# Cosine attention and an MLP mixer on one core: regrouped early slots, epsilon as a two-column sum, zero blocks on GpSimd, and channel weights in pieces of another shape

## The chip, the core and the metric

One core of one Trainium2 chip runs the kernel. The metric is the device time of one execution in microseconds (us). Six runs of the kernel before took 402.56 to 405.12 us, median 404.44 us. In the text TensorE is PE, VectorE is DVE, ScalarE is ACT, GpSimd is POOL and SyncE is SP, as the profile names them.

## The reference, cut to what matters

```
# q, k, v: (8, 12, 448, 64) float32;  tau = 0.1
q_n = q / (norm(q, axis=-1) + 1e-06)
k_n = k / (norm(k, axis=-1) + 1e-06)
attn = softmax(q_n @ k_n.T / tau)
x = (attn @ v) -> (8, 448, 768)              # the 12 heads side by side
h = relu(x.T @ w_tok1) @ w_tok2              # 448 -> 256 -> 448
u = x + h.T
out = u + relu(u @ w_ch1) @ w_ch2            # 768 -> 1536 -> 768
```

The change touches the norms, the epsilon that is added to them, the scaling of q and k, the load of `w_ch1`, and the order of work while the first batch is in flight.

## The kernel before, in words

The work is cut into 48 pairs of heads, six for each of the eight batches. Pair i is handled in slot i, and a slot works on several pairs at once: it scores pair i, multiplies the softmax of pair i-1 with v, runs the token mixer for older pairs, and prepares q and k of later ones. Slots 0 to 5 belong to batch 0, where the sequence is laid out as 112 partitions by 4 chunks. Slot 6 is written out by hand, and slots 7 to 47 run in a loop; from pair 6 on k and v are laid out as 128 rows by 3 chunks and a rest of 64 rows (`kr`, `vr`), which two heads share.

The order of work on every engine is the order in which the program is written: each engine runs its own instructions in that order, and waits at each for what it needs. What a pair goes through:

- `load_qk`, `load_v` (SP): loads in float32. SP is one queue too; it also issues the transposing DMA of `tok2` (line 399) that makes `ut` out of `u` for pairs 0, 1 and 2.
- `square` (POOL or ACT), `sums` (line 253, DVE): squares and their sum over the 64 elements of a row.
- `norms`: Ln and Exp on ACT give the square root; then either DVE adds epsilon (line 262) and takes the reciprocal (line 263), or, with `act=True`, ACT does both by two more activations (lines 268, 269). The early slots use DVE.
- `scale` (line 280): q and k times the reciprocal norm, into the float16 tile `kq`; on POOL except for the first pairs. From pair 6 on the rest of k takes two more multiplications of 64 partitions by 64 elements (line 288), into a block of zeros that DVE sets for pairs 6 to 9 (line 285).
- `tpose` (line 304, PE, and a copy to `qk` by DVE, line 306), or from pair 12 on a transposing DMA.
- `score` (line 327, PE; the exponential on ACT, line 328), `pv` (line 366; division on DVE, lines 369 and 370), `tok1`, `tok2` (PE; DVE lines 382 and 396), `upose` (line 405, PE, for pairs 3 to 5), and `warm`, which are matmuls without a use of their own.
- `m_ch1` (line 415), `m_ch2` (line 430): the channel mixer. From slot 7 on these units fill PE between the other steps, from a queue with a share for each slot. That share is worked out from column counts when the program is built. The first one needs `ut` of all six pairs of batch 0.

PSUM tiles come from two rings in the order in which they are asked for: tag "s" has three buffers (scores, and the token mixer where `wide`), tag "b" has two (transposes, `pv`, `warm`, `upose`). `kq` has four buffers. The weights `w_ch1` (768 by 1536 float32, stored as float16 in `wc1t`) come by four DMAs that POOL issues in slots 2 to 5, each of all six row tiles by 384 columns; the first unit of the channel mixer needs columns 0 to 127 of all row tiles. `w_ch2` comes by two DMAs of six row tiles by 768 columns each, issued in slot 8.

Of the kernel before, what the change touches and what calls it, by code (L numbers as in the profile page):

```python
# [22 lines left out]
def kernel(  # L23
# [169 lines left out]
                              in_=w2n[:].rearrange("p t (s c) -> p t c s", c=NCH))  # L193

    def weights_ch1(i):
        lo, hi = 384 * i, 384 * (i + 1)
        nc.gpsimd.dma_start(out=wc1t[:, :, lo:hi],
                            in_=moe_w_ch1[:, lo:hi].rearrange("(t p) c -> p t c", p=128))

    def weights_ch2():  # L200
        for i in range(2):
# [6 lines left out]
    sqs = [cst.tile([128, 2 * QS, E], FP32, name=f"sq{i}") for i in range(3)]  # L208
    for kq in kqs:
        nc.vector.memset(kq[96:128, 1].rearrange("p c g e -> p (c g e)"), 0.0)  # L210
    for sq in sqs:
        nc.vector.memset(sq[96:128, KS:KS + QS].rearrange("p c e -> p (c e)"), 0.0)

# [42 lines left out]
    def norms(i0, i1, a0=0, a1=2, dve=False, act=False):  # L256
        h = i0 // HP
        n, sl = some(i0, a0, a1)
        ssq = half[h]["ssq"][0:n, i0 - HP * h:i1 - HP * h, sl]
        rn = half[h]["rn"][0:n, i0 - HP * h:i1 - HP * h, sl]  # L260
        if dve:
            nc.vector.tensor_scalar_add(out=rn, in0=rn, scalar1=EPS_NORM)  # L262
            nc.vector.reciprocal(out=rn, in_=rn)
            return
        nc.scalar.activation(out=rn, in_=ssq, func=AF.Ln, bias=tiny[0:n])
        nc.scalar.activation(out=rn, in_=rn, func=AF.Exp, scale=0.5)
        if act:
            nc.scalar.activation(out=rn, in_=rn, func=AF.Ln, bias=eps[0:n])
            nc.scalar.activation(out=rn, in_=rn, func=AF.Exp, scale=-1.0)  # L269

    def scale(i, a, eng=None):
        st = pipe[i]
        eng = eng or nc.gpsimd
        sl, np_ = lay(i)
        if "kq16" not in st:
            st["kq16"] = kqs[i % 4]
        kq, p = st["kq16"], np_[a]
        rn = half[i // HP]["rn"][:, i % HP, sl[a]]
        n = KC if a == 0 and not old(i) else NCH
        eng.tensor_tensor(out=kq[0:p, a, 0:n].rearrange("p c g e -> p g c e"),  # L280
                          in0=st["kq"[a]][:].rearrange("p (g c) e -> p g c e", g=2),
                          in1=_bcast_free(rn[0:p, 0:2 * n].rearrange("p (g c) -> p g c", g=2), E), op=ALU.mult)
        if n == KC:
            if i < NPAIR + 4:
                nc.vector.memset(kq[:, 0, KC].rearrange("p g e -> p (g e)"), 0.0)
            for g in range(2):
                p = slice(64 * g, 64 * g + 64)
                eng.tensor_tensor(out=kq[p, 0, KC, g], in0=half[i // HP]["kr"][p, i % HP],
                                  in1=_bcast_free(rn[p, 2 * KC], E), op=ALU.mult)

    def scaled(i):
        scale(i, 0)
# [195 lines left out]
    with tc.manual_schedule():  # L488
        for i in range(3):
            load_qk(i)  # L490
        load_v(0)
        load_qk(3)
        load_v(1)
        load_qk(4)
        load_v(2)
        load_qk(5)
        load_v(3)
        weights_tok1()
        weights_tok2()

        square(0, 1, act=True)
        square(0, 0, act=True)
        sums(0, 1, 2)
        norms(0, 1, 1, 2)
        sums(0, 0, 1)
        norms(0, 1, 1, 2, dve=True)
        norms(0, 1, 0, 1)
        scale(0, 1, nc.vector)
        norms(0, 1, 0, 1, dve=True)
        scale(0, 0, nc.vector)  # L510
        square(1, 1, act=True)
        square(1, 0, act=True)
        square(2, 1, act=True)
        warm(40, True)
        tpose(0, 1, 2)
        warm(3, True)
        tpose(0, 0, 1)
        warm(5, True)
        square(2, 0)
        sums(1)  # L520
        score(0, 0)
        norms(1, 2)
        norms(1, 2, dve=True)
        score(0, 1)
        scale(1, 0)
        scale(1, 1, nc.vector)
        sums(2)
        cast_v(0)
        score(0, 2)
        warm(14)  # L530
        score(0, 3)
        warm(6)
        tpose(1)
        warm(6)
        norms(2, 3)
        norms(2, 3, dve=True)
        square(3, 1, act=True)
        square(3, 0)
        load_v(4)
        load_qk(6)  # L540

        for i in range(1, NPAIR + 1):
            b, pj = i // NPAIR, i % NPAIR
            if i < NPAIR:
                if i == 1:
                    scale(2, 0)
                    scale(2, 1, nc.vector)
                else:
                    scaled(i + 1)
                    weights_ch1(i - 2)  # L550
                score(i, 0)
                score(i, 1)
                sums(i + 2)
                norms(i + 2, i + 3)
                if i >= 2:
                    tok1(i - 2, wide=True)
                pv(i - 1, 0)
                norms(i + 2, i + 3, dve=True)
                cast_v(i)
                square(i + 3, 0)  # L560
                if i == 1:
                    warm(10)
                tpose(i + 1)
                score(i, 2)
                if i >= 2:
                    tok2(i - 2, pe=(i == NPAIR - 1), wide=True)
                pv(i - 1, 1)
                score(i, 3)
                warm(8)
                square(i + 3, 1, act=True)  # L570
                if i == 1:
                    place_w2()
                load_v(i + 4)
                load_qk(i + 6)
                continue
            load_qk(12)
            load_qk(13)
            scaled(7)
            score(i, 0)
            score(i, 1)  # L580
            sums(8)
            norms(8, 9)
            score(i, 2)
            upose(i - 3)
            tok1(i - 2, wide=True)
            pv(i - 1, 0)
            norms(8, 9, dve=True)
            cast_v(i)
            load_v(i + 4)
            squares(9)  # L590
            score_rest(i)
            tpose(i + 1)
            pv(i - 1, 1)
            tok2(i - 2, pe=True)
            tok1(i - 1, wide=True)
            tok2(i - 1, pe=True)

        def side(i):
            early = i < 12
            if i + 7 < NP_ALL:  # L600
                load_qk(i + 7)
            if i == 8:
                weights_ch2()
            cast_v(i)
            if i + 4 < NP_ALL:
                load_v(i + 4)
            if early:
                for t in SU_AT[i]:
                    sums(t)
                for n in sorted({t // HP for t in SU_AT[i]}):  # L610
                    ts = [t for t in SU_AT[i] if t // HP == n]
                    norms(ts[0], ts[-1] + 1, act=True)
                for t in SC_AT[i]:
                    scaled(t)
                    if t >= DMA_T0:
                        tpose_dma(t)
            for t in SQ_AT[i] if early else [i + 5]:
                if t < NP_ALL:
                    squares(t)
            if not early:  # L620
                if i + 4 < NP_ALL:
                    sums(i + 4)
                    if (i + 4) % HP == 2:
                        norms(i + 2, i + 5, act=True)
                if i + 2 < NP_ALL:
                    scaled(i + 2)
                    tpose_dma(i + 2)
        for i in range(NPAIR + 1, NP_ALL):
            b, pj = i // NPAIR, i % NPAIR
            for c in range(KC):  # L630
                score(i, c)
            pv_rest(i - 1)
            pv(i - 1, 0)
            pv(i - 1, 1)
            if i == NPAIR + 1:
                upose(NPAIR - 2)
                upose(NPAIR - 1)
                refill(0)
            elif pj == 2 and b > 1:
                refill(b - 1)  # L640
            side(i)
            fed[0] += fed[1]
            unit(True)
            score_rest(i)
            if i > NPAIR + 1:
                tok2(i - 2)
            if i + 1 < DMA_T0:
                tpose(i + 1)
            if due():
                unit(True)  # L650
            while due():
                unit()
            tok1(i - 1)
        last = NP_ALL - 1
        pv_rest(last)
        pv(last, 0)
        pv(last, 1)
        tok2(last - 1)
        unit()
        tok1(last)  # L660
        unit()
        tok2(last)
        refill(B - 1)
        while queue:
            unit()
# [35 lines left out]
```

## Time and profile before

| what | value |
|---|---|
| median of six runs | 404.44 us (402.56 to 405.12) |
| the profiled execution | 402.56 us, span 400.7 us |
| PE busy | 377.8 us, 94% of the span |
| DVE, ACT, POOL busy | 211.5, 227.2, 235.5 us (53%, 57%, 59%) |
| chain that ended last, by engine | PE 80%, DVE 8%, DMA 4%, ACT 4%, POOL 2% |
| time of the slots' first score | slot 1 14.5, slot 2 19.6, slot 3 25.0, slot 4 29.7, slot 5 34.5, slot 6 39.6, slot 7 46.5, slot 8 55.3, slot 9 65.7 us |
| data moved | 65.26 MB, HBM read 43.45 MB |

The profile's page gives the busy share of each engine over the span, then the same in 40 slices of 10 us, then DMA queues, then the chain of work that ended last. A line of the timeline has the start and the length in us, the engine, the line of the kernel, the operation with output and inputs, and in brackets the idle time of the engine before it with the operation that ended that idle time. Where several are merged, the length is that of all. Lengths of neighbours overlap a little, so the distance of two starts is what an instruction costs its engine.

### The profile page before, as it was taken

What the parts mean: (1) busy time and instruction counts of PE and PEld (TensorE: products, weight loads), DVE (VectorE), ACT (ScalarE), POOL (GpSimd) and SP (SyncE); (2) the same over time, 40 slices, a digit from 0 to 9 for tenths busy, and PEclk for the clock granted to TensorE, in tenths of its full rate; (3) what the DMA queues carried; (4) which work ended last, traced back from release to release, by engine and by line L of the source; (5) the groups of instructions that cost most, each with busy time, mean ns of one, the idle gap of its engine ahead of it and who ended that gap; (6) DMA issues with size and microseconds to landing.
All of it is one profiled execution on the core that took longest, in us unless ns stands there. A gap on an engine that the chain in (4) does not pass through costs nothing.

```text
span 400.7 us, 10277 instructions
## 1 busy us (share of the span) xinstructions
PE 377.8 (94%) x4126; PEld 245.9 (61%) x4126; DVE 211.5 (53%) x452; ACT 227.2 (57%) x392; POOL 235.5 (59%) x399
## 2 busy tenths in 40 slices
PE   7788779989999999999999999999999999999995
PEld 5566545556656666666666666666666666655562
DVE  7799754566634756447435566356444553332031
ACT  5988665876477536756476455764684446511400
POOL 7898579994959394776849292958666440000000
PEclk9999998999999999999999999999999999999999
DMA  8999999999798868786798779696895472013022
GB/s 211 256 191 187 190 218 230 250 185 197 148 203 213 199 162 195 192 168 147 177 209 165 201 173 216 150 174 141 182 223 118 91 167 67 15 37 108 0 75 84
DMA packets 121535, 65.26 MB, mean 163 GB/s; under 512 B 77584, under 2 KB 117904, under 8 KB 121488
## 3 DMA queue, kind: packets, MB, share of 16 engines
q1 hardware_dynamic: 115872, 59.40, 68.1%
q0 software_dynamic: 5616, 5.21, 8.7%
q8 instruction: 32, 0.52, 0.6%
q14 instruction: 15, 0.12, 0.1%
HBM read 43.45 MB, written 11.01 MB: 136 GB/s over the span
## 4 chain that ended last, share of the span: by engine, by line
PE 80%; DVE 8%; DMA 4%; ACT 4%; POOL 2%; issue 1%; SPq 0%; DVEq 0%; POOLq 0%; ACTq 0%
PE psF L430 27%; PE psG L415 26%; PE psO L366 8%; PE psS L327 6%; PE psU L393 4%; PE psR L379 4%; DMA ut<-u 3%; DVE ssq L253 2%; PE psQ L334 2%; DVE x L370 1%; PE psO L349 1%; POOL kq L280 1%; ACT pt L328 1%; DVE ost L434 1%; DVE rn L262 1%; DMA kf<-in_k_dram 1%
## 5 line engine op out<-in xcount | busy, mean ns | idle before, releaser
L328 ACT ACTIVATE pt<-psS 128x896 f16<-128x896 f32 (+1 forms) x150 | 127.7, 918 | 57.5 <-PE psS L327 57.4
L415 PE MATMUL psG<-ut,wc1t 128*128 128x448 f16 x576 | 118.2, 355 | 0.4 <-DMA ut<-u 0.2
L430 PE MATMUL psF<-wc2t,gt 128*128 128x384 f16 x672 | 115.9, 326 | 0.2 <-ACT gt L418 0.2
L430 PEld LDWEIGHTS <-gt 128*128 128x128 f16 x672 | 63.6, 98 | 39.0 <-issue 0.3
L418 ACT ACTIVATE gt<-psG 128x448 f16<-128x448 f32 x96 | 51.4, 542 | 60.3 <-PE psG L415 60.1
L280 POOL TENSOR_TENSOR kq<-kf,rn 128x384 f16<-128x384 f32 (+1 forms) x47 | 41.0, 872 | 74.0 <-ACT rn L269 72.0
L415 PEld LDWEIGHTS <-wc1t 128*128 128x128 f16 x576 | 54.3, 98 | 45.7 <-issue 2.1
L434 DVE TENSOR_TENSOR ost<-psF,u 128x384 f32<-128x384 f32 (+1 forms) x64 | 35.6, 557 | 63.9 <-PE psF L430 62.3
L253 DVE TENSOR_REDUCE ssq<-sq 128x15 f32<-128x960 f32 (+2 forms) x49 | 55.3, 1131 | 2.4 <-ACT sq L239 2.3
L382 DVE TENSOR_SCALAR rt<-psR 128x256 f16<-128x256 f32 x48 | 20.2, 420 | 62.8 <-PE psR L379 62.6
L280 POOL TENSOR_TENSOR kq<-qf,rn 112x512 f16<-112x512 f32 x45 | 47.0, 1045 | 3.3
L366 PE MATMUL psO<-vt,pt 128*128 128x65 f16 (+1 forms) x1200 | 46.8, 193 | 0.1
L327 PE MATMUL psS<-qk 64*128 64x448 f16 x300 | 40.7, 358 | 3.4 <-ACT gt L418 1.7
L366 PEld LDWEIGHTS <-pt 128*128 128x128 f16 (+1 forms) x1200 | 40.7, 97 | 3.0 <-PE psS L327 0.4
L370 DVE TENSOR_TENSOR x<-psO,rec 128x256 f16<-128x256 f32 x96 | 40.7, 424 | 3.3
L241 POOL TENSOR_TENSOR sq<-qf 112x512 f32<-112x512 f32 x39 | 40.5, 1039 | 0.0
L241 POOL TENSOR_TENSOR sq<-kf 128x384 f32<-128x384 f32 (+1 forms) x46 | 38.9, 845 | 1.3 <-DMA kf<-in_k_dram 1.3
L369 DVE RECIPROCAL rec<-psO 128x4 f32<-128x4 f32 x96 | 16.9, 176 | 38.8 <-PE psO L366 38.7
L396 DVE TENSOR_TENSOR u<-psU,x 128x512 f16<-128x512 f32 x48 | 32.9, 685 | 6.0 <-PE psU L393 4.4
L335 ACT ACTIVATE pt<-psQ 128x448 f16<-128x448 f32 x42 | 22.6, 538 | 17.9 <-PE psQ L334 17.9
L379 PEld LDWEIGHTS <-w1t 128*128 128x128 f16 x384 | 25.5, 99 | 9.8 <-issue 2.1
L393 PEld LDWEIGHTS <-w2t 128*128 128x128 f16 x384 | 25.1, 98 | 9.2 <-issue 1.4
(53 smaller groups left out, 287.5 us busy)
## 6 DMA issues: line engine op xcount, KB each, us to landing
qf<-in_q_dram SPq DMA_DIRECT2D x48, 224.0 KB, 3.9
kf<-in_k_dram SPq DMA_DIRECT2D x42, 192.0 KB, 3.7
vf<-in_v_dram SPq DMA_DIRECT2D x42, 192.0 KB, 3.6
out_dram<-ost SPq DMA_DIRECT2D x8, 336.0 KB, 3.5
wc1t<-in_moe_w_ch_dram POOLq DMA_DIRECT2D x4, 576.0 KB, 9.9
wc2t<-in_moe_w_ch_dram POOLq DMA_DIRECT2D x2, 1152.0 KB, 15.1
out_dram<-ost SPq DMA_DIRECT2D x8, 288.0 KB, 3.0
out_dram<-ost SPq DMA_DIRECT2D x8, 240.0 KB, 3.5
```

Source lines behind the costliest of these rows:

```text
L241: nc.gpsimd.tensor_mul(out=dst, in0=src, in1=src)
L253: nc.vector.tensor_reduce(out=half[i // HP]["ssq"][0:n, i % HP, sl], in_=pipe[i]["sq"][0:n, sl], axis=AXX.X, op=ALU.add)
L280: eng.tensor_tensor(out=kq[0:p, a, 0:n].rearrange("p c g e -> p g c e"), in0=st["kq"[a]][:].rearrange("p (g c) e -> p g c e", g=2), in1=_b ...
L327: nc.tensor.matmul(psS[:, hh, 0:S], qk[hb, c * n:c * n + 128], qm[hb], start=True, stop=True)
L328: nc.scalar.activation(out=pts[i % 2][0:n, 2 * S * c:2 * S * (c + 1)].rearrange("p (h s) -> p h s", h=2), in_=psS[0:n, :, 0:S], func=AF.Ex ...
L366: nc.tensor.matmul(psO[:, m, 0:E + 1], pts[i % 2][0:n, at:at + 128], vt[0:n, i % HP, nch * hh + c, 0:E + 1], start=(old(i) and c == 0), st ...
L370: nc.vector.tensor_tensor(out=st["x"][:, :, hh * E:(hh + 1) * E], in0=psO[:, :, 0:E], in1=_bcast_free(rec[:], E), op=ALU.mult)
L379: nc.tensor.matmul(psR[:, tt], w1t[:, w1[m], tt * 128:(tt + 1) * 128], st["x"][:, m], start=(m == 0), stop=(m == 3))
L393: nc.tensor.matmul(psU[:, m], w2t[:, tt, lo:lo + 128], st["rt"][:, tt], start=(tt == 0), stop=(tt == TT - 1))
L415: nc.tensor.matmul(psG[:, 0:S], wc1t[:, dt, ct * 128:(ct + 1) * 128], ut[b][:, dt].rearrange("p m s -> p (m s)")[:, lo:lo + S], start=(dt ...
L418: nc.scalar.activation(out=gt[:, ct, (b % 2) * S:(b % 2 + 1) * S], in_=psG[:, 0:S], func=AF.Relu)
L430: nc.tensor.matmul(psF[:, 0:DH], gt[:, ct, lo:lo + 128], wc2t[:, ct, dh * DH:(dh + 1) * DH], start=(ct == 0), stop=(ct == CT - 1))
```

## The change

It has five parts.

1. In `norms`, the Exp on ACT of the early slots writes into the first column of a new tile `ne` whose second column holds epsilon; DVE then adds the two columns by a `tensor_reduce` in place of `tensor_scalar_add`.
2. In `scale`, the zero block is set by the engine that scales (POOL), and the two multiplications of the rest of k become `tensor_scalar` with a scalar for each partition, in place of `tensor_tensor` with a broadcast.
3. In slots 1 to 5, the fourth score follows the third, ahead of `tok2` and the second `pv`.
4. In slot 6, the three scores and both `pv` come first, `upose` and `tok1` later, and the norms of pair 8 are wholly on ACT.
5. The pieces of `w_ch1` are three row tiles by 768 columns.

```
     def weights_ch1(i):
-        lo, hi = 384 * i, 384 * (i + 1)
-        nc.gpsimd.dma_start(out=wc1t[:, :, lo:hi],
-                            in_=moe_w_ch1[:, lo:hi].rearrange("(t p) c -> p t c", p=128))
+        cols, t = slice(768 * (i // 2), 768 * (i // 2) + 768), 3 * (i % 2)
+        nc.gpsimd.dma_start(out=wc1t[:, t:t + 3, cols],
+                            in_=moe_w_ch1[128 * t:128 * t + 384, cols].rearrange("(t p) c -> p t c", p=128))
...
+    nes = [cst.tile([128, 2 * QS, 2], FP32, name=f"ne{i}") for i in range(3)]
+    for ne in nes:
+        nc.vector.memset(ne[:, :, 1], EPS_NORM)
...
+        ne = nes[i0 % 3][0:n, sl]
         if dve:
-            nc.vector.tensor_scalar_add(out=rn, in0=rn, scalar1=EPS_NORM)
+            nc.vector.tensor_reduce(out=rn[:, 0], in_=ne, axis=AXX.X, op=ALU.add)
             nc.vector.reciprocal(out=rn, in_=rn)
             return
         nc.scalar.activation(out=rn, in_=ssq, func=AF.Ln, bias=tiny[0:n])
-        nc.scalar.activation(out=rn, in_=rn, func=AF.Exp, scale=0.5)
+        nc.scalar.activation(out=rn if act else ne[:, :, 0], in_=rn if act else rn[:, 0], func=AF.Exp, scale=0.5)
...
             if i < NPAIR + 4:
-                nc.vector.memset(kq[:, 0, KC].rearrange("p g e -> p (g e)"), 0.0)
+                eng.memset(kq[:, 0, KC].rearrange("p g e -> p (g e)"), 0.0)
             for g in range(2):
                 p = slice(64 * g, 64 * g + 64)
-                eng.tensor_tensor(out=kq[p, 0, KC, g], in0=half[i // HP]["kr"][p, i % HP],
-                                  in1=_bcast_free(rn[p, 2 * KC], E), op=ALU.mult)
+                eng.tensor_scalar(out=kq[p, 0, KC, g], in0=half[i // HP]["kr"][p, i % HP],
+                                  scalar1=rn[p, 2 * KC:KS], scalar2=1.0, op0=ALU.mult, op1=ALU.mult)
...
                 score(i, 2)
+                score(i, 3)
                 if i >= 2:
                     tok2(i - 2, pe=(i == NPAIR - 1), wide=True)
                 pv(i - 1, 1)
-                score(i, 3)
                 warm(8)
...
             score(i, 1)
+            score(i, 2)
             sums(8)
-            norms(8, 9)
-            score(i, 2)
-            upose(i - 3)
-            tok1(i - 2, wide=True)
+            norms(8, 9, act=True)
             pv(i - 1, 0)
-            norms(8, 9, dve=True)
+            pv(i - 1, 1)
             cast_v(i)
             load_v(i + 4)
             squares(9)
+            upose(i - 3)
+            tok1(i - 2, wide=True)
             score_rest(i)
             tpose(i + 1)
-            pv(i - 1, 1)
             tok2(i - 2, pe=True)
             tok1(i - 1, wide=True)
             tok2(i - 1, pe=True)
```

## The prediction, made before the changed kernel ran

> **What bounds the kernel now.** The page first: the share of PE in 40 slices of 10 us, and beside it POOL, the granted clock and DMA.
>
> ```profile
> PE   7788779989999999999999999999999999999995
> ...
> POOL 7898579994959394776849292958666440000000
> PEclk9999998999999999999999999999999999999999
> DMA  8999999999798868786798779696895472013022
> ```
>
> From about 90 us to the end PE is full, and the change leaves its work there as it is: a microsecond won before then should reach the end whole. The edits act in the first 75 us, and for 60 of them PE is at 7 or 8 tenths. So I read who stands in PE's way there. The chain of work that ended last, in order of time:
>
> ```profile
> 22.22 1.42 DVE rn L262
> ...
> 27.59 0.80 DVE rn L262
> ...
> 32.38 0.76 DVE rn L262
> ...
> 37.23 13.12 DMA ut<-u
> 50.39 0.92 PE psG L415 x4
> 52.24 1.05 POOL kq L280
> ...
> 59.84 1.05 POOL kq L280
> ```
>
> Three different things: an addition of 16 numbers on DVE; a transfer; then POOL's scaling. The timelines of POOL and PE, and L262's own answer (ns, least/median/most):
>
> ```profile
> L262 DVE TENSOR_SCALAR rn<-rn x10: 165/560/1428, 5.8 to 43.2; 112x16 f32<-112x16 f32 x5, 128x15 f32<-128x15 f32 x3, 112x8 f32<-112x8 f32 x2
> ```
> ```profile
> 22.55 1.04 POOL L241 TENSOR_TENSOR sq<-kf 112x512 f32<-112x512 f32 x1
> 24.07 1.04 POOL L280 TENSOR_TENSOR kq<-kf,rn 112x512 f16<-112x512 f32 x1 [0.48 <-DVE rn L263]
> ...
> 51.51 0.65 POOL L288 TENSOR_TENSOR kq<-kr,rn 64x64 f16<-64x64 f32 x2 [2.80 <-PE psQ L334]
> 52.24 1.04 POOL L280 TENSOR_TENSOR kq<-qf,rn 112x512 f16<-112x512 f32 x1
> 53.25 0.83 POOL L241 TENSOR_TENSOR sq<-kf 128x384 f32<-128x384 f32 x1
> ```
> ```profile
> 59.82 0.23 PE L304 MATMUL pst<-id,kq 128*128 128x128 f16 x1 [0.91 <-POOL kq L288]
> 60.95 0.40 PE L304 MATMUL pst<-id,kq 128*128 128x128 f16 x4 [0.89 <-POOL kq L280]
> 61.18 3.84 PE L415 MATMUL psG<-ut,wc1t 128*128 128x448 f16 x12
> ```
>
> L262 that starts at 22.20 ends at 23.63, just as POOL's square ends (22.55+1.04=23.59); alone it takes 0.17. The reader is to see the same end in the others: 17.51+0.73 beside a square ending 18.21, 27.59+0.79 beside 28.34, 32.34+0.79 beside 33.09. The wait of 2.80 at 51.51 is put down to PE, but what came last is DVE's memset (L285) at 51.26+0.11, queued behind DVE's `ut` copies and a 1.14 us sum.
>
> **Part 1, the epsilon.** Removed: six L262 in 14-40 us: 0.39, 0.73, 1.43, 0.79, 0.79, 0.74, sum 4.87. Added: six reductions of 32 elements. Here two rules pull apart. "VectorE: DVE Perf Modes" (the perf-mode tier table) has `tensor_reduce` at one element per cycle only and float32 `tensor_scalar` at twice that: a reason against the swap. "SBUF — State Buffer" (Who interferes with whom) says a two-port mode takes the pair of ports shared with GpSimd exclusively, and that a trn2 `tensor_reduce` never does. The rows: L253 at 112x1024 takes 1.213 us and at 128x960 1.153, so 0.94 ns per element and 0.25 fixed; 32 elements are 0.28 (estimate). By the first rule alone the six cost 6 x (0.28-0.17)=+0.7 us; by the lock they save 4.87-1.7=3.2 us of DVE. L253 is never stretched though POOL runs beside it, so I take the second. Bounds: -4 and +0.7.
>
> Not all of it shows, because POOL is next. Per slot, by distance of starts in slots 3 and 4 (period 4.75): POOL 4.53 of work; PE about 4.3 with `warm`; ACT 4.2; DVE 4.03 after the cut. So POOL sets about 4.5. What ends is POOL's own idle between 15 and 39.5 us: 0.22 (of 0.40), 0.48, 0.22, 0.22, and 0.86 at 35.25 waiting for the memset: 2.0 us.
>
> **Part 2, zero block and rest of k.** POOL gains a memset of 128x128 float16, 0.20 by its own rows at L144 and L173: -0.2 in slot 5. The pointer `tensor_scalar` on POOL has no row. Nearest: the same 64x64 as `tensor_tensor`, 0.29; a cast of 128x384 takes 0.50 where two inputs take 0.83, so one input less would save 0.05 of 64 elements. I take 0.29, no change; bounds 0.2 and 1.0 each. Gains: the 2.80 idle before pair 8's rest goes, and 0.85 before pair 9's. In slot 7 PE then needn't wait 0.55+0.89=1.44 (rows at 52.22 and 53.34).
>
> **Part 3, scores in twos.** No work. ACT's idle before the fourth exponential (0.33-0.44 per slot, <-PE psS) goes, but ACT isn't the bound; `tok2` and `pv` come 0.3 later on PE, and DVE's `u` behind them, inside DVE's half microsecond of slack. The "s" ring no longer has a score behind DVE's `u`. Zero; bounds -0.5 and +0.5.
>
> **Part 4, slot 6.** PE waits 0.63+0.23+0.57 there. After: on DVE both `pv` evacuations stand behind `sums(8)`, which waited for ACT's square until 40.71 and takes 1.15; `upose` needs a "b" buffer, so PE waits some 0.5, and `tok2` for `rt` about 0.6. ACT gets two more activations (0.31+0.22) where it idled 2.99 us before slot 7. I take -0.3; bounds -0.9 and +0.6.
>
> **Part 5, weights.** The DMA queue rows, 21-51 us and 62-74 us (packets, MB, share of 16 engines):
>
> ```profile
> q0 software_dynamic: 3136, 2.36, 61.7%
> ```
> ```profile
> q0 software_dynamic: 1097, 1.64, 74.7%
> ```
>
> The first is nearly all ch1 (768 B packets): 0.617x16x30/3136=94 ns each. The second is nearly all ch2, whose rows are 768 columns as ch1's will be (1536 B): 0.747x16x12/1097=131 ns. ch1 now takes 3072x94/16=18.1 us of all engines, afterwards 1536x131/16=12.6: 5.5 us less in 21-51. POOL's four issues at 0.89 may fall towards w2n's 0.77: -0.2. The first unit needs pieces 0 and 1, issued by 26 us, landed by 36 even at 9.4: no wait.
>
> **Where the stalls go.** With POOL as bound, slot 6 starts 2.0 (+0.2-0.2) earlier, slot 7 2.3. Then transfers matter. kr of pair 9 landed at 46.2 (POOL waited 1.28+1.32 for kf and kr), `ut` of pair 2 at 50.35, kf of pair 10 at 53.2, just as POOL squared it (53.25). They move with SP, which sat 8.1 us in three waits for `u`, so by about 2; and by the fourth ch1 piece, 1.4 of the 5.5, which lies behind the last gap in DMA at 38 us: 3.4. Then `ut` lands at 47.0 where PE wants it at 50.39-0.24-2.3, about 47.8; slot 7 keeps its 1.44. kf of pair 10 at 49.8; POOL then squares (2.0), issues ch2 (1.7), casts (0.5), scales pair 9 (0.8+0.2+0.65+1.0): 56.7, before 60.9. That is 4.2 earlier; PE comes 3.7 earlier, so slot 8 adds 0.5 and PE still idles about 1.3.
>
> That idle matters for the clock. In 1 us stretches it reads 1.00 at 61, 0.52, 0.50, 0.50, 0.77 from 62: half speed for 3.4 us after PE idled 1.80 in the 3.4 before. "TensorE: Matmul & The Clock Gate" (table in Part 1) has it cold after a window of about 3.4 us that is idle; by that rule this drop would not be. The row decides: half idle is enough. It cost 3.84-2.43 (the same 12 matmuls at 76.28) and 0.31 on psR: 1.7 us. With 1.3 idle it should stay up, but then PE meets POOL at pair 10's transposes, where slack is 0.8 (POOL done 68.2, PE 68.99): +0.8.
>
> Sum: 2.0+0.3+1.44+0.5+0.8=5.0. I hold back 1.0, since three transfers have under a microsecond of margin. 4.0 saved: the profiled 402.56 becomes 398.6; the median is 1.9 above it, so 400.4.
>
> **Rivals.**
> - All margins hold and PE's clock and POOL both keep up to slot 11: 5.0 and the 1.3 idle: -6.3, 398.1. Chance 0.10. Speaks for it: 5.5 us of DMA go. Against: POOL is full in 60-90.
> - Transfers keep their times. Then `ut` at 50.35 holds PE, which only avoids 1.44; and kf at 53.2 holds POOL: pair 9 is done 0.65+0.1 earlier. 0.7 saved: 403.7. Speaks for it: DMA is at 9 tenths all along. Chance 0.20, half of it faster, half within 0.3%.
> - The change doesn't do what it says: the reduction is stretched like L262, so the port wasn't the cause. Of part 1's 2.0 only the memset's wait ends (0.86-0.2): 0.66+0.3+1.44+0.5+0.8=3.7, less the 1.0 held back: 401.7. Against: L253 is never stretched. Chance 0.05.
> - Slower: the pointer multiplication on POOL. It is 2 per pair, 10 for pairs 6 to 10 while POOL is full and on the path. It eats the 4.0 at 0.29+0.4=0.7 us each; at 1.0 each it adds 7.1, so 3.1 slower: 407.5. Against: nothing of that size on POOL takes over 0.34. Chance 0.15.
> - The likeliest, 398.9 to 402.2: 0.50.
>
> 0.3% is 1.2 us, about what this kernel's measurement can tell from none. Faster 0.50+0.10+0.10+0.05=0.75, same 0.10, slower 0.15. Range 398.0 to 405.0: it leaves out a part of the first rival and most of the slower one.
>
> **What would show it.** L267 at 0.2-0.3 us whatever POOL does; POOL without idle in 19-37 us; slot 6's first score at 37.6; no idle before the rest of pair 8; `ut` landing by 48; no half clock at 62. Wrong if POOL's kr rows exceed 0.5 us, or if PE waits over 1.5 us for `ut` or for pair 9's scaling.

## The result and the profile after

The changed kernel takes 401.1 us (median of 19 runs, 397.35 to 406.29) where the kernel before, run beside it, takes 403.92 us (40 runs, 400.9 to 406.85). The ratio is 0.9926, with a 95% interval of 0.9903 to 0.9948: it is faster, by 2.8 us where 4.0 were forecast. Ratios, here and below, leave out executions that took over 1.5% longer than the fastest of their kernel (three of these 19), while the medians are of all, so the two can differ a little. Both kernels spread over some 6 us and more from one execution to the next, twice the gain. The profiled executions happen to lie on the wrong sides: 402.56 us for before (1.4 below its median) and 402.63 for after (1.5 above), with spans of 400.7 and 400.6. So the two traces cannot be subtracted as wholes; they are read stage by stage, and the times come from the medians.

The page of the changed kernel, the same four rows as before: busy tenths in slices of 10 us.

```profile
PE   6888779969999999999999999999999999999995
...
POOL 6899689993959394776849392958766450000000
PEclk9899999989999999999999999999999999999998
DMA  8999999989798859885788879676895382013022
```

POOL reads 9 in the slice from 30 us where it read 8, and 6 and 8 in the two after that where it read 5 and 7. The 8 of the clock in the slice from 60 has gone. It has not vanished from the execution: there is an 8 in the slices from 10 and from 80. The chain of work that ended last, in order of time (start, length, what):

```profile
35.68 1.06 POOL kq L285
...
41.26 10.47 DMA kf<-in_k_dram
...
57.88 1.05 POOL kq L285
...
80.18 4.06 DMA qk<-kq
```

The three additions of DVE have left it. Ahead of 25 us it runs through loads, and from there to 37 us through POOL, as the forecast had it; then it comes, by way of the exponentials on ACT, to the load of k of pair 10, in which it stands 10.5 us. Part 1's line, now a reduction (ns, least/median/most), and POOL's timeline:

```profile
L267 DVE TENSOR_REDUCE rn<-ne x9: 161/184/187, 5.8 to 36.5; 112x16 f32<-112x32 f32 x5, 112x8 f32<-112x16 f32 x2, 128x15 f32<-128x30 f32 x2
```
```profile
24.99 1.04 POOL L285 TENSOR_TENSOR kq<-kf,rn 112x512 f16<-112x512 f32 x1
...
29.40 1.03 POOL L285 TENSOR_TENSOR kq<-kf,rn 112x512 f16<-112x512 f32 x1
...
45.30 0.82 POOL L245 TENSOR_TENSOR sq<-kf 128x384 f32<-128x384 f32 x1 [2.56 <-DMA kf<-in_k_dram]
...
48.55 0.20 POOL L290 MEMSET kq<- 128x128 f16 x1
48.85 0.70 POOL L293 TENSOR_SCALAR kq<-kr,rn 64x64 f16<-64x64 f32 x2
...
51.80 0.83 POOL L245 TENSOR_TENSOR sq<-kf 128x384 f32<-128x384 f32 x1 [1.12 <-DMA kf<-in_k_dram]
```

The same scaling comes 4.41 us apart, where the period was 4.75, and none of POOL's rows from 20.6 to 42.4 us has a bracket: POOL is the bound of the early slots and no longer waits for DVE. At 48.85 there is no bracket either, where before it read 2.80. But at 45.30 and 51.80 POOL waits for k of pairs 9 and 10, and those are the loads that should have landed 3.4 us earlier.

PE in slots 7 and 8:

```profile
50.74 0.40 PE L309 MATMUL pst<-id,kq 128*128 128x128 f16 x4 [0.57 <-POOL kq L285]
...
58.98 0.40 PE L309 MATMUL pst<-id,kq 128*128 128x128 f16 x4 [0.90 <-POOL kq L285]
59.22 2.43 PE L420 MATMUL psG<-ut,wc1t 128*128 128x448 f16 x12
```

The 12 matmuls take 2.43 us at full clock, where they took 3.84, most of it at half.

### The profile page after: what moved, and what is told of

It reads as the page before. It is cut to its first block, busy times and chain, and to the rows that moved or that the text cites. A ratio compares the mean times of both kernels' runs of the same rounds, so it can differ in the third digit from the quotient of the medians.

```text
span 400.6 us, 10277 instructions
## 1 busy us (share of the span) xinstructions
PE 376.1 (94%) x4126; PEld 244.9 (61%) x4126; DVE 209.5 (52%) x449; ACT 227.5 (57%) x394; POOL 238.7 (60%) x403
## 4 chain that ended last, share of the span: by engine, by line
PE 77%; DMA 10%; POOL 5%; DVE 3%; ACT 2%; issue 1%; SPq 1%; POOLq 0%; ACTq 0%
PE psF L435 26%; PE psG L420 25%; PE psO L371 8%; PE psS L332 6%; PE psU L398 4%; PE psR L384 4%; DMA kf<-in_k_dram 3%; DMA qf<-in_q_dram 2%; DMA vf<-in_v_dram 2%; POOL kq L285 2%; DMA kr<-in_k_dram 2%; PE psQ L339 2%; POOL sq L245 1%; PE psO L354 1%; DMA qk<-kq 1%; DVE ost L439 1%
## 5 line engine op out<-in xcount | busy, mean ns | idle before, releaser
L420 PE MATMUL psG<-ut,wc1t 128*128 128x448 f16 x576 | 116.6, 352 | 0.2 <-ACT gt L423 0.2
L435 PEld LDWEIGHTS <-gt 128*128 128x128 f16 x672 | 63.7, 98 | 39.1 <-issue 0.5
L420 PEld LDWEIGHTS <-wc1t 128*128 128x128 f16 x576 | 53.9, 98 | 44.6 <-issue 0.3
L257 DVE TENSOR_REDUCE ssq<-sq 128x15 f32<-128x960 f32 (+2 forms) x49 | 55.3, 1132 | 2.9 <-ACT sq L243 2.8
L371 PE MATMUL psO<-vt,pt 128*128 128x65 f16 (+1 forms) x1200 | 47.2, 194 | 0.0
L371 PEld LDWEIGHTS <-pt 128*128 128x128 f16 (+1 forms) x1200 | 41.2, 98 | 3.4 <-PE psS L332 0.7
L398 PEld LDWEIGHTS <-w2t 128*128 128x128 f16 x384 | 25.1, 98 | 9.8 <-issue 2.4
L398 PE MATMUL psU<-rt,w2t 128*128 128x128 f16 x384 | 29.3, 219 | 1.1 <-DVE rt L387 0.8
```

The lines of the kernel that those rows point to most:

```text
L257: nc.vector.tensor_reduce(out=half[i // HP]["ssq"][0:n, i % HP, sl], in_=pipe[i]["sq"][0:n, sl], axis=AXX.X, op=ALU.add)
L371: nc.tensor.matmul(psO[:, m, 0:E + 1], pts[i % 2][0:n, at:at + 128], vt[0:n, i % HP, nch * hh + c, 0:E + 1], start=(old(i) and c == 0), st ...
L398: nc.tensor.matmul(psU[:, m], w2t[:, tt, lo:lo + 128], st["rt"][:, tt], start=(tt == 0), stop=(tt == TT - 1))
L420: nc.tensor.matmul(psG[:, 0:S], wc1t[:, dt, ct * 128:(ct + 1) * 128], ut[b][:, dt].rearrange("p m s -> p (m s)")[:, lo:lo + S], start=(dt ...
L435: nc.tensor.matmul(psF[:, 0:DH], gt[:, ct, lo:lo + 128], wc2t[:, ct, dh * DH:(dh + 1) * DH], start=(ct == 0), stop=(ct == CT - 1))
```

## The experiments

Each kernel was timed beside the kernel before, and its ratio is to that. Three questions were put. **Which parts gain?** (each alone, then each undone.) **What ends the gain that the early slots made?** The theory: the loads that SP issues, held by the transposing DMAs of `ut`. Its rivals: pair 12's transposing DMA at 80 us, which ends the chain above; the `w_ch2` transfers; and the price of part 2. **Would the loads alone have been enough?**

### One part at a time

Part 1 alone: the first column of `ne`, and the reduction.

```
-            nc.vector.tensor_scalar_add(out=rn, in0=rn, scalar1=EPS_NORM)
+            nc.vector.tensor_reduce(out=rn[:, 0], in_=ne, axis=AXX.X, op=ALU.add)
```

> The kernel before with part 1 alone (epsilon as a two-column reduction). Theory A (the addition waited for POOL's port): the reduction takes 0.16 to 0.19 us wherever it stands, slot 6 begins 1.0 to 1.5 us earlier than 39.6, but POOL still idles for DVE's memset at pairs 8 and 9, so 1 to 2 us are left at the end (ratio 0.995 to 0.998). Theory B (the gain is made by the lighter weights, part 5): within 0.1% of before.

Measured: 401.55 us, ratio 0.9957 (0.9936 to 0.9977). Slot 6 starts at 38.0 us instead of 39.6, a little more than the 1.0 to 1.5 expected. The reduction takes 161 to 188 ns in all ten places.

The zero block alone, moved to POOL (the multiplications stay as they were):

```
-                nc.vector.memset(kq[:, 0, KC].rearrange("p g e -> p (g e)"), 0.0)
+                eng.memset(kq[:, 0, KC].rearrange("p g e -> p (g e)"), 0.0)
```

> The kernel before with only the zero block set by POOL instead of DVE. Theory A: POOL's idle of 0.86, 2.80 and 0.85 us before the rest of k of pairs 6, 8 and 9 goes; slot 9 begins 1 to 2 us earlier; at the end 0.5 to 1.5 us (ratio 0.996 to 0.999). Theory C (whatever is won before 80 us ends in the wait for pair 12's transposing DMA, which lands at about 84.3): slot 12 begins no more than 1.2 us earlier, so half of it at most is seen.

Measured: 402.86 us, ratio 0.9958 (0.9932 to 0.9983). In its trace no wait is left on POOL before the rest of k; it waits 2.39 and 2.79 us for loads of k of pair 9 instead.

Part 5 alone, the pieces of `w_ch1`:

```
-        nc.gpsimd.dma_start(out=wc1t[:, :, lo:hi],
+        nc.gpsimd.dma_start(out=wc1t[:, t:t + 3, cols],
```

> The kernel before with only the weight pieces of part 5. Theory B: 1 to 3 us faster, because transfers land 2 to 4 us earlier from 40 to 56 us. Theory A: early slots are set by DVE and POOL, so slot 6 begins as before, and only waits for transfers (0.24 and 2.6 us of POOL in slot 6 and 7) shrink; 0 to 1 us, ratio 0.998 to 1.000.

Measured: 404.17 us, ratio 0.9998 (0.9973 to 1.0023): nothing.

Parts 3 and 4 alone, the order:

```
                 score(i, 2)
+                score(i, 3)
                 if i >= 2:
                     tok2(i - 2, pe=(i == NPAIR - 1), wide=True)
                 pv(i - 1, 1)
-                score(i, 3)
...
-            norms(8, 9)
...
+            norms(8, 9, act=True)
```

> The kernel before with only the new order of slots 1 to 6 (parts 3 and 4); pair 8's norms are wholly on ACT. By my prediction it is worth 0.3 us, so no difference that can be measured (ratio 0.998 to 1.001). A rival: since tok2 and pv come later on PE, DVE's queue behind the stretched addition gets longer, and it is slower by 0.5 us.

Measured: 402.92 us, ratio 0.9979 (0.9960 to 0.9997): a small gain, at the edge of what could be told from none, where none was expected.

The single gains are 0.43, 0.42, 0.02 and 0.21%, in sum 1.08%. Together they give 0.74%. The intervals are too wide to call this sum wrong, but it is no sum that grows.

### The whole, and one part undone at a time

The changed kernel once more, with nothing edited, for a second trace:

> The changed kernel once more, unedited, beside the three below. Ratio 0.990 to 0.995. Its trace tells whether slot 12's wait for pair 12's transposing DMA (3.77 us in the first trace) is there in other executions: by theory C it is, 1.5 to 4 us, since that DMA is issued at about 80 us whatever came before; if it was an accident of one execution, under 1 us.

Measured: 400.73 us, ratio 0.9915 (0.9886 to 0.9944). This trace shows best what is gained and lost. Slot 6 starts at 37.6, the very time that the forecast gave; then slot 7 takes 12.7 us where it took 8.8 before, and slot 8 starts at 57.3, 2.0 later than before. The row of POOL in slot 7:

```profile
48.27 0.82 POOL L245 TENSOR_TENSOR sq<-kf 128x384 f32<-128x384 f32 x1 [5.63 <-DMA kf<-in_k_dram]
```

Half of the 3.9 us that slot 7 loses is the clock: PE is busy for 8.44 us of it, at a mean granted clock of 0.81, where it was busy for 6.48 before at full clock. The other half is idle time of PE, 4.29 us where it was 2.29.

Without part 1 (the addition as it was):

```
-            nc.vector.tensor_reduce(out=rn[:, 0], in_=ne, axis=AXX.X, op=ALU.add)
+            nc.vector.tensor_scalar_add(out=rn, in0=rn, scalar1=EPS_NORM)
```

> The changed kernel with the epsilon added by tensor_scalar again (part 1 undone). Theory A: the addition is stretched again to 0.4 to 1.4 us, slot 6 begins 1 us or more later than in the changed kernel, and 1 to 2 us of the gain are lost (ratio 0.995 to 0.998). Theory C: slots before 80 us move, but slot 12 begins at the same time, since the transfer sets it: the ratio stays near that of the changed kernel.

Measured: 401.74 us, ratio 0.9951 (0.9927 to 0.9975). In its trace the addition takes up to 1067 ns again. Slots 1 to 5 take 23.9 us, as long as in the first trace of the changed kernel and 1.0 longer than in the second. By the times, part 1 is worth 0.25 to 0.36% on top of the rest (0.9951 against the 0.9926 and 0.9915 of the changed kernel; the intervals overlap).

Without part 5:

```
-        nc.gpsimd.dma_start(out=wc1t[:, t:t + 3, cols],
+        nc.gpsimd.dma_start(out=wc1t[:, :, lo:hi],
```

> The changed kernel with the old weight pieces (part 5 undone). By my prediction part 5 lets kf and kr of pair 9 and ut land 1.4 us earlier: undone, 0.5 to 1.5 us of the gain go (ratio 0.993 to 0.997). Alone it gave nothing (0.9998), so by theory D: as the changed kernel, 0.990 to 0.994, with kf of pair 9 at 44 to 48 us as before.

Measured: 400.76 us, ratio 0.9911 (0.9891 to 0.9932). Undone it costs nothing, as it gained nothing alone.

Without parts 3 and 4:

```
-                score(i, 3)
                 if i >= 2:
                     tok2(i - 2, pe=(i == NPAIR - 1), wide=True)
                 pv(i - 1, 1)
+                score(i, 3)
...
-            norms(8, 9, act=True)
+            norms(8, 9)
...
+            norms(8, 9, dve=True)
```

> The changed kernel with the old order of slots 1 to 6 (parts 3 and 4 undone). I predicted that the order is worth 0.3 us; alone it measured 0.9979, some 0.8 us. If the order and the reduction answer the same wait (ACT's or DVE's idle in the early slots), it costs nothing on top of part 1: 0.991 to 0.993. If it is worth 0.8 us of its own, 0.993 to 0.995.

Measured: 401.03 us, ratio 0.9926 (0.9896 to 0.9955): the order gives 0.2% alone, and beside the other parts nothing that can be told.

### The rivals for what ends the gain

Pairs 12 and 13 transposed by PE, so that no transposing DMA stands before slot 12:

```
-    DMA_T0 = 12
+    DMA_T0 = 14
```

> The changed kernel with pairs 12 and 13 transposed by PE and DVE instead of by DMA (DMA_T0 14 instead of 12). Theory C: slot 12 no longer waits and begins about 3 us earlier, at 81 to 82 us; PE pays 2 x 0.45 us; 1.5 to 3 us faster than the changed kernel (ratio 0.984 to 0.990). If the wait is not what holds the rest: as the changed kernel or 0.9 us slower.

Measured: 400.75 us, ratio 0.9945 (0.9924 to 0.9967), no better than 0.9926 and 0.9915, though slot 12 begins at 82.5 in its trace. The wait of 3.77 us at slot 12 in the first trace of the changed kernel is a matter of that execution: in the second trace this DMA was issued at 77.8, landed at 83.7, and slot 12 began at 84.6 without waiting for it (PE waited 1.28 us there for ACT, as in the kernel before).

`w_ch2` issued a slot later:

```
-            if i == 8:
+            if i == 9:
                 weights_ch2()
```

> The changed kernel with the load of the second channel weights issued one slot later (slot 9). It tells what delays pair 12's transposing DMA. If it is the load of these weights that fills the DMA engines from 54 to 76 us ahead of it, the loads of slots 8 to 10 land earlier, but the weights end later, and the DMA for pair 12 is issued at about the same time: no difference (0.99 to 0.996). If the place in SP's queue alone sets it, also none. If PE meets ch2 before its weights have landed (about 80 us), slower by 1 us or more.

Measured: 401.65 us, ratio 0.9948 (0.9929 to 0.9967): no gain. k of pair 9 landed at 46.1, so it was late without these transfers.

The transposing DMAs of `ut` taken out: pairs 0 to 2 of batch 0 transposed by PE and copied by DVE, as pairs 3 to 5 are.

```
-                    tok2(i - 2, pe=(i == NPAIR - 1), wide=True)
+                    tok2(i - 2, pe=True, wide=True)
...
+            upose(0)
+            upose(1)
             tok2(i - 1, pe=True)
...
+                upose(2)
                 upose(NPAIR - 2)
```

> The changed kernel with ut of pairs 0, 1 and 2 made by PE transposes and DVE copies in slots 6 and 7, as pairs 3 to 5 are, instead of by three transposing DMAs in slots 2 to 4. Theory D (the gain of the early slots is lost again to loads that land late behind the transposing DMAs, whose share of the queue leaves holes of 2 to 4 us in which the DMA engines move under 80 GB/s): the holes at 36 to 46 us go, kf of pair 9 lands before 43 us instead of 45 to 48, slot 8 begins at 50 to 52 us, ratio 0.980 to 0.988. If the holes have another cause: they stay, PE and DVE pay 3 x (0.24 + 0.41), ratio 0.990 to 0.996.

Measured: 394.74 us (six runs, 394.36 to 397.07), ratio 0.9780 (0.9751 to 0.9809), though PE and DVE have more to do. POOL's row at the same place, and the next rest of k:

```profile
43.55 0.83 POOL L245 TENSOR_TENSOR sq<-kf 128x384 f32<-128x384 f32 x1
...
46.80 0.21 POOL L290 MEMSET kq<- 128x128 f16 x1
```

No bracket on either: k of pair 9 had landed at 39.0. Slot 8 began at 53.4, later than expected, and the ratio is still a little below the range of theory D. How the loads came to be late is seen on SP's own timeline. First the kernel before: the load of k of pair 9, and the third transposing DMA.

```profile
34.16 1.15 SPq L112 DMA_DIRECT2D kf<-in_k_dram  x1
...
37.23 2.60 SPq L399 DMA_TRANSPOSE ut<-u  x1
```

The same two in the second trace of the changed kernel, and the second transposing DMA ahead of them:

```profile
28.62 1.66 SPq L404 DMA_TRANSPOSE ut<-u  x1
...
31.57 0.58 SPq L112 DMA_DIRECT2D kf<-in_k_dram  x1
...
35.13 8.10 SPq L404 DMA_TRANSPOSE ut<-u  x1
```

The load is issued 2.6 us earlier and lands, by POOL's row, at 48.2 instead of 44.0: 16.6 us after its issue instead of 9.8. And SP stays in the third transposing DMA for 8.10 us, with every later load behind it; it was not waiting for that pair's `u`, which DVE had written by 32.1. But k of pair 9 is not among the later loads: SP had issued it 3.6 us before, so it was late after its issue, not because SP was held. What stands ahead of it is the second transposing DMA, which landed 11.3 us after its issue, at 39.9 (9.6 us in the kernel before). The held SP delays k of pair 10, issued at 44.89 instead of 42.08. In nine traces (both of the changed kernel, part 1 alone, the zero block alone, and those without part 1, without part 5, without parts 3 and 4, with pairs 12 and 13 on PE and with `w_ch2` later) the third transposing DMA held SP for 3.1 to 8.1 us; in the kernel before, and with the weights alone or the order alone, for 2.6 to 2.7. What the DMA engines did meanwhile, in a stretch of 5 us (the last two columns are DMA's share and GB/s), in the second trace of the changed kernel and then with `ut` by PE:

```profile
35.00:40.00 5.00, 4.19 (x78) 3.03 (x78) 3.26 (x8) 4.01 (x6) 3.58 (x7) 1.00 1.06 73
```
```profile
35.00:40.00 5.00, 4.39 (x77) 3.15 (x76) 4.42 (x13) 4.33 (x9) 4.73 (x10) 1.00 1.16 251
```

The engines are called busy in both (1.06 and 1.16 of their time), but the first moves 73 GB/s and the second 251. That share of busy time, which the forecast read as "9 tenths all along", says nothing of what is moved here.

### Are the loads enough?

The same edit made to the kernel before, with nothing of the change:

```
-                    tok2(i - 2, pe=(i == NPAIR - 1), wide=True)
+                    tok2(i - 2, pe=True, wide=True)
...
+            upose(0)
+            upose(1)
...
+                upose(2)
```

> The kernel before with one thing added that is not part of the change: ut of pairs 0 to 2 is transposed by TensorE in slots 6 and 7 in place of the three transposing DMAs of slots 2 to 4. Theory H (those DMAs leave holes in the queue that bound slots 7 and 8 by themselves, whatever the early slots do): kf of pair 9 lands before 41 us, slot 8 begins before 54.0 us, and the ratio to the kernel before is 0.980 to 0.990. Theory J (the holes only bind once the early slots are faster, so the change and this edit need each other): slot 8 stays at 54.5 to 55.5 us, ratio 0.992 to 0.998. If H holds and the ratio is 0.985, the change on top of it (0.978 together) is worth 0.7%, as much as it was worth alone; if J holds it is worth 1.4 to 2.0%, which is the 4 to 8 us that it was expected to give.

Measured: 403.81 us (22 runs), ratio 1.0000 (0.9977 to 1.0023). Theory H is right about the transfer (k of pair 9 lands at 36.9 us) and wrong about the time; theory J has the side, but not the size, and its reason is another than the one it gave. POOL and DVE in slot 7 of this kernel show why:

```profile
54.20 0.65 POOL L288 TENSOR_TENSOR kq<-kr,rn 64x64 f16<-64x64 f32 x2 [6.39 <-DVE kq L285]
```
```profile
51.60 1.32 DVE L406 COPY ut<-psT 128x512 f16<-128x512 f16 x3
52.84 1.14 DVE L253 TENSOR_REDUCE ssq<-sq 128x15 f32<-128x960 f32 x1
53.94 0.11 DVE L285 MEMSET kq<- 128x64 uint32 x1
```

POOL had its k early, did its work, and then stood 6.39 us before the rest of pair 8, waiting for a memset of 0.11 us that is queued on DVE behind the copies of `ut` and a sum. The run with part 5 alone has the same wait with the transposing DMAs in place. There k of pair 9 landed 8.9 us after its issue, POOL did not wait for it, and the time stayed (0.9998):

```profile
52.64 0.65 POOL L288 TENSOR_TENSOR kq<-kr,rn 64x64 f16<-64x64 f32 x2 [5.72 <-DVE kq L285]
```

That memset comes 5.1 us after slot 7's first score in the kernel before with `ut` by PE (53.94-48.8), and 4.8 after it both in the kernel before (51.26-46.5) and with part 5 alone (52.38-47.6): it moves with the slot, not with the loads. So two waits lie one behind the other at the same place. With the change alone the memset is gone and the load is last; with `ut` by PE alone the load is early and the memset is last; only without both does POOL run through. On top of `ut` by PE the change is worth 0.978/1.000, or 2.2% (about 1.8 to 2.6), some 8.9 us, against 2.8 by itself.

The starts of the slots in the five traces (us), with the end of the span:

| trace | slot 1 | slot 6 | slot 7 | slot 8 | slot 9 | slot 12 | end | k of pair 9 landed | pair 8 scaled |
|---|---|---|---|---|---|---|---|---|---|
| before | 14.5 | 39.6 | 46.5 | 55.3 | 65.7 | 85.4 | 400.7 | 44.0 | 53.3 |
| changed, first | 15.2 | 39.1 | 45.3 | 52.7 | 62.0 | 84.3 | 400.6 | 45.2 | 50.7 |
| changed, second | 14.7 | 37.6 | 44.6 | 57.3 | 64.8 | 84.6 | 400.0 | 48.2 | 53.7 |
| changed, `ut` by PE | 16.8 | 39.9 | 46.5 | 53.4 | 60.4 | 80.2 | 395.2 | 39.0 | 48.9 |
| before, `ut` by PE | 15.5 | 41.2 | 48.8 | 57.9 | 68.3 | 88.1 | 403.1 | 36.9 | 56.0 |

The last column is the end of the scaling of pair 8's q, POOL's last step for it. In the three changed kernels it comes 5.4 us after POOL begins to square k of pair 9 (45.30, 48.27, 43.55), since between the two POOL has only its own work; in the two others the memset sets it. The last two rows show where the change gains on top of `ut` by PE. It begins slot 1 1.3 us later, then saves 2.6 us in slots 1 to 5, 1.0 in slot 6, 2.2 in slot 7 and 3.4 in slot 8: 7.9 by slot 12. So the memset, which acts in slots 7 and 8, is not the whole of it; and of the 3.4 some 1.7 is a half clock that only the last row's trace has in slot 8 (the 12 matmuls took 3.74 us there, psR 1.02 instead of 0.61). From slot 12 to the end all five take 315.0 to 316.3 us: what is decided is decided before 85 us.

## Why the forecast was right, and where its step failed

The forecast was faster, 400.4 us with 398.0 to 405.0; measured, 401.1. The sign and the mechanism of the first two parts hold. The size of part 5 did not, and with it failed the step by which the loads were to land 3.4 us earlier. That the total came near all the same is in part luck: the 1.0 us that I held back stood against 2.2 that were lost.

**Part 1: right.** The reduction takes 0.16 to 0.19 us beside whatever POOL does, where the addition took up to 1.43. Of the two rules that pulled apart, the Trainium skill's "SBUF — State Buffer" (Who interferes with whom) is the one that the trace follows; the loss that "VectorE: DVE Perf Modes" (the perf-mode tier table) would make of it is not to be seen at this size, 0.18 for 32 elements where the addition of 16 took 0.17 alone. My 0.28 was too much, since the fixed part of L253's line does not carry over to a small tile. Slots 1 to 6: the second trace begins slot 6 at 37.6, exactly 2.0 earlier. The first begins it at 39.1: its slot 1 is 0.7 later than before, and slots 1 to 5 take 23.9 us instead of 25.1 (22.9 in the second). The rival in which the reduction is stretched is out.

**Part 2: right in size.** The memset takes 0.20. The pointer multiplication on all its 84 places, against the two-input form in the kernel before (ns, least/median/most):

```profile
L293 POOL TENSOR_SCALAR kq<-kr,rn x84: 307/317/321, 34.9 to 323.3; 64x64 f16<-64x64 f32 x84
```
```profile
L288 POOL TENSOR_TENSOR kq<-kr,rn x84: 282/289/293, 35.2 to 323.3; 64x64 f16<-64x64 f32 x84
```

It is 0.03 us dearer: ten of them cost 0.3 us, far from the 7.1 of the slower rival, which is out. The wait of 2.80 and the two on the memset are gone. In slot 7 of the first trace PE still waits 0.57 of its 1.44.

**Parts 3 and 4: in their bounds,** with no sure gain beside the other parts: 0.9926 without them, 0.9926 and 0.9915 with them.

**Part 5: wrong in size.** The packets did fall as counted. The row of the weights' queue, 21 to 51 us, in the changed kernel, and with `ut` by PE:

```profile
q0 software_dynamic: 1600, 2.36, 59.3%
```
```profile
q0 software_dynamic: 1600, 2.36, 47.2%
```

The first is 0.593x16x30/1600=178 ns for a packet of mostly 1536 bytes, the second 142, near the 131 that I took. In the kernel before with `ut` by PE the row reads 53.9% for 3136 packets, or 82 ns where I took 94. So, as far as these rows show, the 94 held time that packets lose beside the transposing DMAs, and the 131, from another stretch, did not: I compared unlike rows. With those DMAs gone the new shape saves 2.0 us of all engines (53.9 against 47.2%), not 5.5; with them the share falls from 61.7 to 59.3%, or to 49.5% with part 5 alone, whose time stays (0.9998). What was saved reached nobody.

**The step that failed: "They move with SP ... and by the fourth ch1 piece ...: 3.4."** SP did move: the load of k of pair 9 was issued 2.3 us earlier in the first trace and 2.6 in the second. But I took its time from issue to landing as constant, less 1.4. It rose from 9.8 to 13.3 and 16.6 us. The load landed at 45.2 and 48.2, where the step needed 40.6; k of pair 10 came at 51.7 and 51.0, not at 49.8. `ut` of pair 2 landed at 47.3 and 49.1, not at 47.0. So for these loads the rival "transfers keep their times" (chance 0.20) is nearer than my likeliest case: k of pair 9 came even later than before, k of pair 10 by 1.5 and 2.2 earlier. What that costs differs. In the first trace slots 6, 7 and 8 still save 0.7, 1.4 and 1.1 us, near the 0.3, 1.4 and 1.3 of the sum; in the second slot 7 alone loses 3.9, half of it by the clock, PE waits 1.37, 0.60 and 0.84 for POOL and 0.88 for `ut` in it, and slot 8 wins 2.9 back. The median of 401.1, between the rival's 403.7 and the 399.4 that 5.0 us would have given, is presumably what such executions make together: the 1.0 that I held back for transfers was the right thought and should have been 2.2. What lengthens the loads was shown by taking out the three transposing DMAs; I had named their landing, for `ut`, but not what they do to the loads in the same queue.

**Slots 8 and 9, and the clock.** No half clock follows slot 8 in the first trace, though PE waits 0.77+0.60+0.90=2.3 us there, where I called for 1.3 and named over 1.5 as a sign of error. My reading that half idle is enough was near, but I took the idle time of whatever 3.4 us lie before. In each trace the clock's changes lie whole multiples of 3.41 us apart, so windows of that length can be laid between them. The window ahead of the drop in the kernel before, then the two over which the 2.3 us fall (length, PE busy, granted clock, DMA share, GB/s):

```profile
58.63:62.04 3.41, 1.61 (x16) 1.00 1.15 212
```
```profile
53.33:56.74 3.41, 2.81 (x49) 1.00 0.71 163
56.74:60.16 3.42, 1.75 (x13) 1.00 1.12 213
```

PE was busy for 0.47 of the first, and for 0.82 and 0.51 of the others. Of 377 such windows at full clock in the 14 traces, from 13 to 110 us, a half clock followed all seven in which PE was busy for less than 0.47, six of the ten between 0.47 and 0.585, and none of the 360 busier ones. So about half busy is the limit in these traces; what decides between 0.47 and 0.585 stays open.

The half clock falls elsewhere instead: at 84.0 to 87.5 in the first trace, 52.6 to 59.4 in the second, 17.4 to 20.8 with `ut` by PE. The stretch of 3.4 us in the kernel before cost some 1.7 (3.84-2.43, and 0.31 on psR), and a wait for a late load can bring one on, as in the second trace. So the 0.8 that I put to its absence in slot 9 cannot be counted as a gain of the change.

**Pair 12's transposing DMA** was not in the forecast. It cost 3.77 us in the first trace, none in the second, and its removal gained nothing.

What stays open: why a transposing DMA holds SP for 1.3 us at one time and 8.1 at another, and why so little is moved around it. Whether the pieces of `w_ch1`, which are moved in the same stretch, have a part in that was not tried; a hole of 28 to 43 GB/s stands at 24 to 26 us also in the trace with `ut` by PE, so not every hole needs a transposing DMA. Nor was it tried which parts of the change the 394.74 us need; that it needs the zero block on POOL is argued from the rows of 6.39 and 5.72 us, not shown by a run.

## What to carry to other kernels

When one engine waits for two things at nearly the same place, take both away before you judge either: here each alone gave 0.0 to 0.7%, and both gave 2.2%. A load that is issued earlier need not land earlier; compare its time from issue to landing with what stands ahead of it in the queue, and look at the bytes moved, not at the engines' busy share. And a short instruction placed on a busy in-order engine (a memset of 0.11 us) costs what is queued ahead of it.

## What the hardware showed that was not expected

A transposing DMA issued by SP took 1.3 us of SP as the first of the three, and 2.6 to 8.1 us as the third, some 10 to 13 us later; from issue to landing it took 4.7 to 14.0 us. Around it the DMA engines moved 58 to 190 GB/s in the worse of the stretches 35 to 40 and 40 to 45 us of the twelve traces with these DMAs, and 222 and 251 in the two without. A multiplication by a scalar for each partition with one tensor input was no cheaper on POOL at 64x64 than one with two tensor inputs (0.317 against 0.289 us). The halved clock came in stretches of 3.4 us, or twice that, in every trace of the table and at different places in each, after windows of 3.41 us in which PE was busy for up to 0.584. It may make a good part of the 6 us by which equal kernels differ: in the 163 executions of the kernel before that ran beside the experiments the time falls as the mean granted clock rises from 0.978 to 0.996 (correlation -0.68). No run separates the two.
